# Attention and MoE on one core: batch 0's norms in one piece, batch 1's k and q cast and copied in other ways, pair 5's scores ahead of unit 4, the last values sooner

## The chip, the core and the metric

The kernel runs on one core of one Trainium2 chip. A core has five engines with a queue of their own, each working strictly in the order in which the program wrote its instructions: TensorE (PE, matrix products, with weight loads listed apart as PEld), VectorE (DVE), ScalarE (ACT), GpSimd (POOL) and SyncE (SP, which here only starts DMAs). They wait for each other by semaphores. Matrix products are written to PSUM banks; the other engines move them on to SBUF. The metric is the device time of one launch in microseconds (us); lower is better. The time before is 324.1 us, the median of three runs (323.36 to 324.86).

## The reference

Eight batches of eight heads, 576 positions, head size 64. First an attention with a window of 128 and a bias that falls with distance, then two matrix products with a gate between them:

```python
scores = scale * np.matmul(q, k.transpose(0, 1, 3, 2))
bias = slopes[:, None, None] * (-np.abs(rel).astype(np.float32))[None, :, :]
mask = (rel >= 0) & (rel < window)
scores = np.where(mask, scores + bias[None], -1000000000.0)
attn = np.exp(scores - np.max(scores, axis=-1, keepdims=True))
attn = attn / (np.sum(attn, axis=-1, keepdims=True) + 1e-09)
x = np.matmul(attn, v)              # then (8*576, 512): 4608 tokens
h = x @ w_in                        # (4608, 2048)
g = h * np.clip(h + 3.0, 0.0, 6.0) / 6.0
out = g @ w_out                     # (4608, 512), float32
```

## The kernel before

**Pairs.** The work of the attention goes by pairs of heads: pair g is heads 2p and 2p+1 of batch b, with g = 4b + p, 32 pairs in all. For batches 0 and 1 a pair's steps are:

- its k and q come in by DMA (`load_double`, two pairs at a time) as float32 in `ldbuf`; a cast to bf16 (`prepare_double`, L246, tile `pr`) is made in two halves, one for the even and one for the odd heads, on an engine that the caller names (V is VectorE, A ScalarE, P GpSimd);
- nine TensorE transposes turn two pairs' k, or q, into one PSUM tile. `wide_double` (L283 to L293) takes one of the two score tiles for it and moves both pairs on with one copy (1152 elements in a partition, L291, to `kTb` or `qTb`); `double` (L255) does it in two parts in other banks;
- `scores_diag` (L331) and `scores_off` (L357 and L363, after the bias tables L342 and L345) write the scores into one score tile each, `exp_diag` and `exp_off_full` (L407, L410, L394) take exponentials on ScalarE, and GpSimd masks what needs it (L412);
- `attend` multiplies by v (L440, L448) into a score tile; VectorE takes a reciprocal (L469) and multiplies by it (L470), which gives the normed values `avs`. `attend_split` does the same by two parts in two other banks, with two reciprocals and two products (L481, L482);
- `back` transposes `avs` on TensorE (L502) and copies the result into `xT`, the input of the first matrix product (L504, L505, L508). From batch 2 on, with two exceptions, a DMA transposes instead (L495).

There are only two score tiles, handed out in turn by `score_banks()`, so a user of one waits until the engine that reads its last content is done.

**Units.** The matrix products are cut into units, which `fill(n)` takes in order, n at a time, and which the program puts between the steps of the attention. An up unit (`moe_up`, four matmuls of 512 columns, L521) makes one 128 by 512 tile of h, ScalarE a relu of it (L545, tile `r`), VectorE the gate (L546, tile `gbuf`). Its PSUM bank comes from the pool "h" (two banks), or for some units of the first tile from "av" or "o" (one each, L535). A down unit (`moe_down`, L576) is a quarter of one 128-row block of the result. `up_begin` and `up_more` start units 0 and 1 of the first tile of tokens before all of `xT` is there. Units that need pairs that aren't done (`done[0]`) are not taken.

**Order.** Everything is in the order of the program text (`manual_schedule` for all engines). `first_batch` does batch 0 and prepares batch 1's first two pairs, `second_batch` does batch 1, and `segment` walks pairs 8 to 31 with a table of fills: at each pair seven numbers f[0] to f[6] say how many units go between which steps. At the last step, g = G = 32, only the values of pair 31 are left: `values` for blocks 0 to 2 (bank "av", reciprocal L458, product L459), `values` for blocks 3 and 4 in the same bank, and `back`, which is a DMA there. The tile of tokens number 7, the last but one, needs that DMA.

**Weights.** The first 512 columns of `w_in` come as float32 and are cast in four pieces (`cast_raw`, L187); the other three parts are DMAs that GpSimd issues (`load_w_in`, L176), the first of them in `second_w_in`.

The lines around the change, as numbered in the profile of the kernel before:

Of the kernel before, what the change touches and what calls it, by code (L numbers as in the profile page):

```python
# [11 lines left out]
BF16 = mybir.dt.bfloat16  # L12
# [6 lines left out]
def kernel(  # L19
# [9 lines left out]
    nc = tc.nc  # L29
    B, H, S, D = q.shape  # L30
# [5 lines left out]
    NP = H // 2  # L36
# [4 lines left out]
    RP, RT = 64, 9  # L41
# [5 lines left out]
    G = B * NP  # L47
# [5 lines left out]
    xT = perm.tile([128, n_ks, RING + SP - S], BF16)  # L53
# [12 lines left out]
    prs = ctx.enter_context(tc.tile_pool(name="prs", bufs=2))  # L66
# [119 lines left out]
    def cast_raw(ks, copy):  # L186
        copy(out=w_in_sb[:, ks, 0:512], in_=raw[:, ks, :])  # L187
# [33 lines left out]
    st = {}  # L221
# [20 lines left out]
    def prepare_double(b, dp, copies, nms="kq", early=None):  # L242
        for nm, copy in zip(nms, copies):
            pr = prs.tile([128, RT, 2 * D], BF16, tag=f"pr{nm}", name="pr2")
            for e in range(2):
                copy(out=pr[:, :, ts(e, D)],  # L246
                     in_=ldbuf["qk".index(nm)][:, ds((2 * dp + e) * RT * D, RT * D)].rearrange(
                         "p (t d) -> p t d", t=RT))
                if early and (nm, e) == (nms[0], 0):
                    early()  # L250
            st[b, dp, nm] = pr

    BANKS = {"h": ps_h, "av": ps_av, "o": ps_o}

    def double(b, dp, nm, part, tag, copy):  # L255
# [25 lines left out]
                         in_=st[b, dp, nm, part].rearrange("p t (a i) -> p i a t", i=2)[:, i])  # L281

    def wide_double(b, dp, nm, copy):  # L283
        src = st[b, dp, nm]
        wide = score_banks()
        tp = wide.rearrange("p s c -> p (s c)").bitcast(BF16)[:, 0:RT * 128].rearrange(
            "p (t c) -> p t c", t=RT)
        for t in range(RT):
            nc.tensor.transpose(tp[:, t, :], src[:, t, :], ident)
        dst = (qTb if nm == "q" else kTb)[b % 2][:, 2 * dp:2 * dp + 2, :, :]  # L290
        copy(out=dst.rearrange("p i j c -> p i (j c)")[:, :, 0:S].rearrange(  # L291
                 "p i (a t) -> p i a t", t=RT),
             in_=tp.rearrange("p t (a i) -> p i a t", i=2))  # L293

    def full(g):
        return g < NB_FULL * NP
# [176 lines left out]
    def attend_split(g, tags):  # L473
        st[g, "avs"] = small.tile([128, NQ, 2, D], BF16, tag="avs", name="avs")
        for tag, qts in zip(tags, ((0, 1, 2), (3, 4))):
            nq = len(qts)
            av = BANKS[tag].tile([128, 3, 2, W], FP32, tag=tag, name="av",
                                 padded_shape=[128, 3, 2, 85])
            av_matmuls(g, qts, lambda qt, e: av[:, qt - qts[0], e, :])
            rc = small.tile([128, 3, 2, 1], FP32, tag="rc", name="rc")  # L480
            nc.vector.reciprocal(rc[:, 0:nq, :, :], av[:, 0:nq, :, D:W])  # L481
            nc.vector.tensor_tensor(  # L482
                out=st[g, "avs"][:, qts[0]:qts[0] + nq, :, :], in0=av[:, 0:nq, :, 0:D],
                in1=rc[:, 0:nq, :, :].to_broadcast([128, nq, 2, D]), op=ALU.mult)
# [6 lines left out]
    def back(g, tag=None):  # L491
        b, hp = divmod(g, NP)
        avs = st[g, "avs"].rearrange("p j e d -> p j (e d)")
        if by_xbar(g):
            nc.sync.dma_start_transpose(  # L495
                out=xT[:, hp, ds(b % 4 * S, SP)].rearrange("p (j c) -> p j c", j=NQ),
                in_=avs.rearrange("p j c -> p (j c)"))
            return
        tag = tag or ("o" if b < 2 else "h")
        tp = BANKS[tag].tile([128, SP], BF16, tag=tag, name="tb", padded_shape=[128, 1024])  # L500
        for j in range(NQ):
            nc.tensor.transpose(tp[:, ts(j, 128)], avs[:, j, :], ident)  # L502
        if g == NP - 1:
            nc.scalar.copy(out=xT[:, hp, ds(b % 4 * S, 256)], in_=tp[:, 0:256])  # L504
            nc.vector.tensor_copy(out=xT[:, hp, ds(b % 4 * S + 256, S - 256)], in_=tp[:, 256:S])  # L505
            return
        eng = nc.vector.tensor_copy if g == 2 * NP - 1 else nc.scalar.copy
        eng(out=xT[:, hp, ds(b % 4 * S, S)], in_=tp[:, 0:S])  # L508

    gts, ops = {}, {}  # L510
# [19 lines left out]
    def up_more(nt, ms, n):  # L530
        hps, k0 = begun[nt, ms]
        up_mms(nt, ms, k0, n, hps)
        begun[nt, ms] = hps, n
# [99 lines left out]
    def first_batch():  # L633
        prepare(0, (V, A))
        load_block(0, "v", 1, nc.scalar)
        for j in (4, 0, 2, 3):
            load_block(0, "v", j, nc.sync)
        load_raw()
        warm_up(5)
        tables_diag(0)  # L640
        tables_off(0)
        transposes(0, (V, A))
        scores_diag(0)
        prepare(1, (P, V))
        transposes(1, (V, V))
        scores_off(0)
        exp_full(0)
        scores_diag(1)
        prepare_double(0, 1, (V, P), "qk")
        tables_off(1)  # L650
        scores_off(1)
        double_begin(0, 1, "q", ("av", "o"))
        double_begin(0, 1, "k", ("h", "h"))
        exp_full(1)
        double_copy(0, 1, "q", 0, (V, V))
        double_copy(0, 1, "k", 0, (A, A))
        scores_diag(2)
        double_copy(0, 1, "q", 1, (V, V))
        double_copy(0, 1, "k", 1, (V, V))
        tables_off(2)  # L660
        scores_off(2)
        exp_full(2)
        scores_diag(3)
        cast_v(0, 4, P)
        cast_v(0, 0, P)
        cast_v(0, 1, P)
        cast_v(0, 2, V)
        cast_v(0, 3, V)
        scores_off(3)
        exp_full(3)  # L670
        attend(0)
        for dp in range(2):
            for nm in "kq":
                load_double(1, dp, nm, nc.sync)
        load_tokens(1, "v")
        attend_split(1, ("av", "h"))
        attend(2)
        back(0, "o")
        cast_raw(0, P)
        cast_raw(1, P)  # L680
        attend(3)
        cast_raw(2, A)
        back(1, "av")
        cast_raw(3, P)
        prepare_double(1, 0, (P,), "k")
        second_w_in()
        up_begin(0, 0, 1)
        up_begin(0, 1, 1)
        back(2, "o")
        prepare_double(1, 0, (V,), "q")  # L690
        up_more(0, 0, 2)
        up_more(0, 1, 2)
        back(3, "av")
        wide_double(1, 0, "k", V)
        wide_double(1, 0, "q", A)
        up_more(0, 0, 3)
        up_more(0, 1, 3)
        done[0] = NP
        fill(2)
        prepare_double(1, 1, (P,), "k")  # L700
        load_w_in(2)
        prepare_double(1, 1, (P,), "q")
        load_w_in(3)
        for dp in range(2):
            for nm in "kq":
                load_double(2, dp, nm, nc.sync)

    def second_batch():
        scores_diag(NP + 0)
        exp_diag(NP + 0, 0)  # L710
        exp_diag(NP + 0, 1)
        fill(2)
        scores_off(NP + 0)
        exp_off_full(NP + 0)
        wide_double(1, 1, "k", V)
        wide_double(1, 1, "q", A)
        fill(2)
        scores_diag(NP + 1)
        exp_diag(NP + 1, 0)
        exp_diag(NP + 1, 1)  # L720
        fill(2)
        scores_off(NP + 1)
        exp_off_full(NP + 1)
        fill(1)
        cast_tokens(1, "v")
        scores_diag(NP + 2)
        exp_diag(NP + 2, 0)
        exp_diag(NP + 2, 1)
        fill(1)
        scores_off(NP + 2)  # L730
        exp_off_full(NP + 2)
        fill(2)
        for i in range(0, 4):
            load_w_out(i)
        g = 2 * NP - 1
        scores(g)
        exp_diag(g, 0)
        exp_diag(g, 1)
        prepare_double(2, 0, (V, P))
        prepare_double(2, 1, (P, P))  # L740
        nc.gpsimd.memset(ldbuf[2][:, 0:1], 0.0)
        load_tokens(2, "v")
        for dp in range(2):
            load_double(3, dp, "k", nc.sync)
        load_tokens(3, "q")
        exp_off_full(g)
        fill(1)
        attend(NP)
        fill(1)
        attend(NP + 1)  # L750
        fill(1)
        back(NP)
        attend(NP + 2)
        fill(1)
        back(NP + 1)
        double(2, 0, "k", 0, "av", A)
        attend(NP + 3)
        back(NP + 2)
        double(2, 0, "k", 1, "av", A)
        wide_double(2, 0, "q", A)  # L760
        up_begin(1, 0, 3)
        back(2 * NP - 1)
        up_begin(1, 1, 3)
        done[0] = 2 * NP
        fill(2)
        scores(2 * NP)

    FILLS = {g: (1, 1, 1, 2, 0, 1, 1) for g in range(9, 15)}

    def segment(lo, hi, fills):  # L770
        for g in range(lo, hi + 1):
# [91 lines left out]
```

## Time and profile before

| what | value |
|---|---|
| median of three runs | 324.1 us (323.36 to 324.86) |
| the profiled execution: its time | 323.67 us |
| its span, first to last instruction | 322.0 us |
| granted TensorE clock over the span | 0.999 |
| busy, share of the span: TensorE | 96% |
| VectorE, ScalarE, GpSimd | 54%, 61%, 43% |
| a relu (L545), a gate (L546), mean of 144 | 690 ns, 686 ns |
| a cast of 128 by 576 float32 (L246): VectorE, GpSimd | 746 ns, 671 ns |
| a copy of 1152 elements (L291): VectorE, ScalarE | 1350 ns, 1121 ns |
| a copy of 576 elements (L239): VectorE, ScalarE | 757 ns, 638 ns |
| L279, VectorE, every other element of a PSUM tile: 320 and 256 elements | 484 ns, 428 ns |

The busy time of an engine says little by itself: TensorE's matmuls are pipelined, and the end of each is modelled, so the starts of successive matmuls tell more than their durations. In a line of the timeline the first number is the start in us from the start of the span, the second how long the group took, and the bracket at the end how long the engine had been idle and what ended it. Instructions that follow each other on ScalarE or VectorE overlap a little: two relus of 0.69 us each take 1.27 us, and the next starts 1.15 us after the first.

### The profile page before, as it was taken

The numbers are of one execution on the slowest core, as the hardware profiler recorded it, in microseconds if no ns is written. First come the engines' busy times: TensorE is split into PE (matmuls) and PEld (weight loads), VectorE is DVE, ScalarE is ACT, GpSimd is POOL, SyncE is SP. The second block draws the span as 40 slices with busy tenths as digits, with TensorE's granted clock in tenths as the row PEclk, the third lists the DMA queues.
The fourth block names the chain that finished last, engine by engine and source line by source line (L and its number), as shares of the span: only waits on it lengthen the run. The fifth ranks groups of instructions, "written<-read, shape, count | busy, mean of one in ns | idle before, by whom it ended". The sixth has DMA issues, their size and how long they took to land.

```text
span 322.0 us, 7006 instructions
## 1 busy us (share of the span) xinstructions
PE 310.5 (96%) x2707; PEld 162.8 (51%) x2707; DVE 174.2 (54%) x345; ACT 197.0 (61%) x338; POOL 138.4 (43%) x247
## 2 busy tenths in 40 slices
PE   6888999999999999999999999999999999999996
PEld 3564465455555444444667644444444444444443
DVE  6776585555346655655555556555656355445510
ACT  3858977777777766766676667666764244244401
POOL 7365491666495666456754664563331000000000
PEclk9999999999999999999999999999999999999999
DMA  7999999989999998999899999943112100000112
GB/s 268 256 373 205 255 245 205 247 210 198 188 259 170 189 243 198 203 219 221 179 174 237 185 205 210 201 120 70 41 34 86 55 34 33 35 33 33 65 51 81
DMA packets 131425, 52.43 MB, mean 163 GB/s; under 512 B 118976, under 2 KB 122816, under 8 KB 131392
## 3 DMA queue, kind: packets, MB, share of 16 engines
q1 hardware_dynamic: 125648, 46.15, 67.3%
q0 software_dynamic: 3696, 3.67, 7.1%
q10 hardware_dynamic: 2048, 2.16, 2.2%
q8 instruction: 21, 0.34, 0.5%
q14 instruction: 12, 0.10, 0.1%
HBM read 36.70 MB, written 9.44 MB: 143 GB/s over the span
## 4 chain that ended last, share of the span: by engine, by line
PE 79%; DMA 7%; ACT 7%; DVE 4%; issue 2%; SPq 0%; DVEq 0%; ACTq 0%
PE ops L576 34%; PE hps L521 34%; PE score L384 3%; ACT r L545 3%; DMA ldbuf<-in_q_dram 3%; DMA xT<-avs 2%; DMA kTb<-tbuf 2%; PE av L448 2%; PE av L440 2%; PE ops L557 1%; DVE gbuf L546 1%; DVE avs L470 1%; ACT gbuf L410 1%; ACT gbuf L394 1%; PE tp L261 1%
## 5 line engine op out<-in xcount | busy, mean ns | idle before, releaser
L546 DVE SCALAR_TENSOR_TENSOR gbuf<-r,hps 128x512 bf16<-128x512 f32 x144 | 98.4, 686 | 103.5 <-ACT r L545 100.1
L545 ACT ACTIVATE r<-hps,bias 128x512 f32<-128x512 f32 x144 | 98.8, 690 | 87.6 <-PE hps L521 87.4
L521 PE MATMUL hps<-xT,w_in_sb 128*128 128x512 bf16 (+1 forms) x640 | 145.2, 358 | 1.4 <-DMA xT<-avs 0.8
L576 PE MATMUL ops<-w_out_sb,gbuf 128*128 128x512 bf16 x560 | 138.0, 379 | 0.0
L521 PEld LDWEIGHTS <-w_in_sb 128*128 128x128 bf16 x640 | 59.1, 98 | 55.7 <-issue 3.4
L576 PEld LDWEIGHTS <-gbuf 128*128 128x128 bf16 x560 | 52.2, 98 | 57.1
L412 POOL TENSOR_SCALAR_AFFINE_SELECT pd<-pd 128x512 bf16<-128x512 bf16 x48 | 29.5, 631 | 38.4 <-ACT pd L410 38.4
L421 POOL TENSOR_SCALAR_AFFINE_SELECT po<-po 128x512 bf16<-128x512 bf16 x48 | 30.1, 632 | 32.2 <-ACT po L419 32.0
L410 ACT ACTIVATE pd<-score,bias_d 128x512 bf16<-128x512 f32 x48 | 31.5, 683 | 5.7 <-PE score L384 5.7
L585 DVE COPY osb<-ops 128x512 f32<-128x512 f32 x33 | 22.7, 687 | 21.5 <-PE ops L576 21.4
L419 ACT ACTIVATE po<-score,bias_o 128x512 bf16<-128x512 f32 x48 | 33.1, 689 | 0.0
L213 POOL CAST tbuf<-ldbuf 128x512 bf16<-128x512 f32 (+1 forms) x45 | 25.5, 611 | 15.7 <-issue 15.7
L459 DVE TENSOR_TENSOR avs<-av,rc 128x384 bf16<-128x384 f32 (+1 forms) x48 | 23.6, 491 | 1.6
L448 PEld LDWEIGHTS <-pd 128*128 128x128 bf16 x192 | 14.3, 97 | 7.9 <-POOL tbuf L213 0.2
L440 PE MATMUL av<-vbuf,po 128*128 128x65 bf16 x192 | 18.0, 193 | 0.0
L448 PE MATMUL av<-vbuf,pd 128*128 128x65 bf16 x192 | 17.3, 193 | 0.0
L440 PEld LDWEIGHTS <-po 128*128 128x128 bf16 x192 | 14.3, 98 | 2.9 <-DVE avs L459 0.5
L424 ACT ACTIVATE p4buf<-score,bias_d 128x64 bf16<-128x64 f32 x48 | 15.6, 324 | 0.0
L206 POOL CAST vbuf<-ldbuf 128x1024 bf16<-128x1024 f32 x14 | 14.2, 1041 | 2.4 <-DMA ldbuf<-in_v_dram 2.4
L384 PEld LDWEIGHTS <-kTb 64*64 64x64 bf16 x480 | 9.4, 106 | 9.5 <-issue 8.5
L384 PE MATMUL score<-qTb,kTb 64*64 64x192 bf16 (+1 forms) x480 | 13.1, 234 | 0.3 <-DMA kTb<-tbuf 0.3
L246 POOL CAST pr<-ldbuf 128x576 bf16<-128x576 f32 x18 | 11.5, 671 | 3.2 <-DMA ldbuf<-in_k_dram 1.7
(108 smaller groups left out, 200.3 us busy)
## 6 DMA issues: line engine op xcount, KB each, us to landing
out_dram<-osb SPq DMA_DIRECT2D x33, 256.0 KB, 2.5
ldbuf<-in_v_dram SPq DMA_DIRECT2D x31, 256.0 KB, 4.9
ldbuf<-in_q_dram SPq DMA_DIRECT2D x20, 256.0 KB, 4.9
ldbuf<-in_k_dram SPq DMA_DIRECT2D x16, 256.0 KB, 4.8
ldbuf<-in_q_dram SPq DMA_DIRECT2D x12, 288.0 KB, 6.3
ldbuf<-in_k_dram SPq DMA_DIRECT2D x12, 288.0 KB, 6.4
w_out_sb<-in_moe_w_out_dram POOLq DMA_DIRECT2D x4, 512.0 KB, 10.5
w_in_sb<-in_moe_w_in_dram POOLq DMA_DIRECT2D x3, 512.0 KB, 10.1
```

The costliest lines, as they stand in the source:

```text
L213: nc.gpsimd.tensor_copy(out=tbuf[:m, :, j, :], in_=s[:m, j, :, :].rearrange("p (i e) d -> p i (e d)", e=2))
L384: nc.tensor.matmul(wide[e][c, ds(at, n)], lhsT=kT[r, j, c], rhs=qT[r, ds(q0, n)], start=True, stop=True)
L410: nc.scalar.activation(out=pd[:, e, :, :], in_=block_scores(g, e, False), func=ACT.Exp, bias=bias_d[:, h:h + 1], scale=scale)
L412: nc.gpsimd.affine_select(out=pd[:, e, :, :], in_=pd[:, e, :, :], pattern=[[0, 4], [1, 128]], channel_multiplier=-1, base=0, compare_op=AL ...
L419: nc.scalar.activation(out=po[:, e, :, :], in_=sc, func=ACT.Exp, bias=bias_o[:, h:h + 1], scale=scale)
L421: nc.gpsimd.affine_select(out=po[:, e, :, :], in_=po[:, e, :, :], pattern=[[0, 4], [-1, 128]], channel_multiplier=1, base=-1, compare_op=A ...
L440: nc.tensor.matmul(out_av, lhsT=po[:, e, (qt if full(g) else qt - 1) % 4, :], rhs=vb[:, qt - 1, h, :], start=True, stop=False)
L448: nc.tensor.matmul(out_av, lhsT=d, rhs=vb[:, qt, h, :], start=(qt == 0), stop=True)
L521: nc.tensor.matmul(hps[:, lo:hi], lhsT=w_in_sb[:, ks, ts(ms, 128)], rhs=xT[:, ks, ds(src, hi - lo)], start=(ks == 0), stop=(ks == n_ks - 1))
L545: nc.scalar.activation(out=r6, in_=hps, func=ACT.Relu, bias=bias3[:, 0:1], scale=1.0 / 6.0)
L546: nc.vector.scalar_tensor_tensor(out=gts[nt][:, ms, :], in0=r6, scalar=1.0, in1=hps, op0=ALU.min, op1=ALU.mult)
L576: nc.tensor.matmul(ops[nt, sub], lhsT=gts[nt][:, ms, ts(sub, 128)], rhs=w_out_sb[:, ms, :], start=(ms == 0), stop=(ms == n_ms - 1))
```

## The change

In `first_batch`: pair 1 is normed in one piece (`attend(1)`, in a score tile) and not by `attend_split`. The pieces of `w_in` are cast by P, A, A, P and not by P, P, A, P. The cast of batch 1's first q moves from VectorE (both halves) to ScalarE (even heads) and GpSimd (odd heads), in the new `prepare_halves`. Its first k and q are no longer copied two pairs at once: the new `wide_begin` does the nine transposes, and the new `wide_copy` moves one pair on, so that pair 4's k goes by VectorE and its q by ScalarE, and pair 5's k and q by VectorE after them. The k transposes stand before `back(3)`, which now copies on VectorE alone. In `second_batch`: the q of pairs 6 and 7 goes by `double` in two parts into banks "o" and "av", copied by VectorE and not by ScalarE; `scores_off(5)` follows `scores_diag(5)` directly, and the units 4 to 8 come after it in one row, where 4 and 5 stood before `scores_diag(5)`, 6 and 7 between the two and 8 behind. At the last step the fills are (1, 0, 1, 0, 0, 1, 2) and not (1, 1, 1, 2, 0, 1, 2): one unit instead of two before the values of blocks 0 to 2, and one instead of three between them and those of blocks 3 and 4. The units left out there come behind.

```diff
@@ first_batch
-        attend_split(1, ("av", "h"))
+        attend(1)
+        back(0, "o")
         attend(2)
-        back(0, "o")
         cast_raw(0, P)
-        cast_raw(1, P)
+        cast_raw(1, A)
+        back(1, "av")
         attend(3)
         cast_raw(2, A)
-        back(1, "av")
-        cast_raw(3, P)
         prepare_double(1, 0, (P,), "k")
         second_w_in()
         up_begin(0, 0, 1)
         up_begin(0, 1, 1)
         back(2, "o")
-        prepare_double(1, 0, (V,), "q")
         up_more(0, 0, 2)
         up_more(0, 1, 2)
+        wide_begin(1, 0, "k")
+        wide_copy(1, 0, "k", 0, 1, V)
+        prepare_halves(1, 0, "q", (A, P))
+        cast_raw(3, P)
         back(3, "av")
-        wide_double(1, 0, "k", V)
-        wide_double(1, 0, "q", A)
         up_more(0, 0, 3)
         up_more(0, 1, 3)
+        wide_begin(1, 0, "q")
+        wide_copy(1, 0, "q", 0, 1, A)
+        wide_copy(1, 0, "k", 1, 1, V)
+        wide_copy(1, 0, "q", 1, 1, V)
@@ second_batch
         wide_double(1, 1, "k", V)
-        wide_double(1, 1, "q", A)
-        fill(2)
+        double(1, 1, "q", 0, "o", V)
+        double(1, 1, "q", 1, "av", V)
         scores_diag(NP + 1)
         exp_diag(NP + 1, 0)
         exp_diag(NP + 1, 1)
-        fill(2)
         scores_off(NP + 1)
         exp_off_full(NP + 1)
-        fill(1)
+        fill(5)
@@ segment's fills
+    FILLS[G] = (1, 0, 1, 0, 0, 1, 2)
@@ the new functions
+    def prepare_halves(b, dp, nm, copies):
+        pr = prs.tile([128, RT, 2 * D], BF16, tag=f"pr{nm}", name="pr2")
+        for e in range(2):
+            copies[e](out=pr[:, :, ts(e, D)], in_=ldbuf[...])
+        st[b, dp, nm] = pr
+    def wide_begin(b, dp, nm):          # the transposes of wide_double
+        ...
+        st[b, dp, nm, "wide"] = tp
+    def wide_copy(b, dp, nm, i, n, copy):   # n pairs from pair i on
+        dst = (qTb if nm == "q" else kTb)[b % 2][:, ds(2 * dp + i, n), :, :]
+        copy(out=..., in_=st[b, dp, nm, "wide"].rearrange("p t (a i) -> p i a t", i=2)[:, ds(i, n)])
@@ back
-        if g == NP - 1:
-            nc.scalar.copy(out=xT[:, hp, ds(b % 4 * S, 256)], in_=tp[:, 0:256])
-            nc.vector.tensor_copy(out=xT[:, hp, ds(b % 4 * S + 256, S - 256)], in_=tp[:, 256:S])
-            return
-        eng = nc.vector.tensor_copy if g == 2 * NP - 1 else nc.scalar.copy
+        eng = nc.vector.tensor_copy if g in (NP - 1, 2 * NP - 1) else nc.scalar.copy
```

More of the change, by code (lines that the diff above doesn't have):

```diff
@@ L251, in prepare_double @@
             st[b, dp, nm] = pr
+    def prepare_halves(b, dp, nm, copies):
+        pr = prs.tile([128, RT, 2 * D], BF16, tag=f"pr{nm}", name="pr2")
+        for e in range(2):
+            copies[e](out=pr[:, :, ts(e, D)],
+                      in_=ldbuf["qk".index(nm)][:, ds((2 * dp + e) * RT * D, RT * D)].rearrange(
+                          "p (t d) -> p t d", t=RT))
+        st[b, dp, nm] = pr
     BANKS = {"h": ps_h, "av": ps_av, "o": ps_o}
@@ L283, in wide_double @@
     def wide_double(b, dp, nm, copy):
+        wide_begin(b, dp, nm)
+        wide_copy(b, dp, nm, 0, 2, copy)
+    def wide_begin(b, dp, nm):
         src = st[b, dp, nm]
@@ L289, in wide_double @@
             nc.tensor.transpose(tp[:, t, :], src[:, t, :], ident)
-        dst = (qTb if nm == "q" else kTb)[b % 2][:, 2 * dp:2 * dp + 2, :, :]
+        st[b, dp, nm, "wide"] = tp
+    def wide_copy(b, dp, nm, i, n, copy):
+        dst = (qTb if nm == "q" else kTb)[b % 2][:, ds(2 * dp + i, n), :, :]
         copy(out=dst.rearrange("p i j c -> p i (j c)")[:, :, 0:S].rearrange(
                  "p i (a t) -> p i a t", t=RT),
-             in_=tp.rearrange("p t (a i) -> p i a t", i=2))
+             in_=st[b, dp, nm, "wide"].rearrange("p t (a i) -> p i a t", i=2)[:, ds(i, n)])
     def full(g):
```

## The prediction

> **What bounds the kernel now.** I read the page's busy shares first, then the busy time by stretches, then each engine's timeline where TensorE (PE) pauses.
>
> ```profile
> PE 310.5 (96%) x2707; PEld 162.8 (51%) x2707; DVE 174.2 (54%) x345; ACT 197.0 (61%) x338; POOL 138.4 (43%) x247
> ```
> ```profile
> 17.00:24.20 7.20, 6.03 (x114) 4.58 (x115) 5.98 (x14) 3.66 (x7) 4.93 (x9) 1.00 1.07 369
> 24.20:32.00 7.80, 6.78 (x63) 3.68 (x61) 4.79 (x6) 6.82 (x10) 4.08 (x7) 1.00 1.25 205
> 32.00:42.00 10.00, 10.00 (x96) 4.74 (x94) 5.70 (x9) 9.98 (x17) 5.75 (x9) 1.00 1.14 278
> 245.00:254.00 9.00, 8.20 (x51) 3.79 (x48) 4.46 (x9) 1.96 (x3) 0.00 (x0) 1.00 0.18 53
> ```
>
> PE is the bound: a gain must come from its pauses, or from nowhere. In the second fence the columns are length, PE, PEld, DVE, ACT, POOL, clock, DMA share and GB/s. PE pauses in 17 to 32 us and near 250; from 32 to 42 ACT is full too (9.98 of 10 us). PE's timeline names the pauses:
>
> ```profile
> 23.71 0.68 PE L289 MATMUL score<-ident,pr 128*128 128x128 bf16 x9 [0.37 <-DVE pr L246]
> ...
> 25.60 0.40 PE L331 MATMUL score<-qTb,kTb 64*128 64x128 bf16 x8 [0.34 <-ACT qTb L291]
> ...
> 29.99 0.66 PE L289 MATMUL score<-ident,pr 128*128 128x128 bf16 x9 [0.68 <-ACT gbuf L394]
> ```
> ```profile
> 22.25 1.41 DVE L246 CAST pr<-ldbuf 128x576 bf16<-128x576 f32 x2
> ...
> 29.68 1.35 DVE L291 COPY kTb<-score 128x1152 bf16<-128x1152 bf16 x1
> ```
> ```profile
> 24.43 1.12 ACT L291 COPY qTb<-score 128x1152 bf16<-128x1152 bf16 x1 [1.17 <-PE score L289]
> ```
>
> The q transposes wait for DVE's cast, pair 4's scores for ACT's copy of both pairs, the second q transposes for a score tile. At the end:
>
> ```profile
> 249.12 0.17 DVE L458 RECIPROCAL rc<-av 128x4 f32<-128x4 f32 x1
> 249.32 0.42 DVE L459 TENSOR_TENSOR avs<-av,rc 128x256 bf16<-128x256 f32 x1
> ```
> ```profile
> 252.15 0.81 PE L521 MATMUL hps<-xT,w_in_sb 128*128 128x512 bf16 x3
> 253.76 1.24 PE L521 MATMUL hps<-xT,w_in_sb 128*128 128x512 bf16 x5 [0.80 <-DMA xT<-avs]
> ```
>
> Three matmuls start 0.215 us apart, so the fourth could start at 252.80 and starts at 253.76: 0.96 us lost, because the last norms end at 249.74 and their DMA takes 3.91.
>
> **Norms in one piece.** `attend(1)` now uses the score tile that pair 3's exponential (16.92 + 1.02) reads until 17.94: it starts at 17.99, not 17.63. DVE's split cost 1.24 us between starts (18.90 to 20.14), in one piece 1.06 (20.14 to 21.20). But pair 2's values now wait for pair 0's norms (18.98) and for `back(0)` (19.04 to 19.33), end at 20.07, and so start the third reciprocal at 20.12: the last norms end at 22.31 against 22.33. Worth nothing; bounds -0.02 and, by the late start, +0.36. I take nothing, as the next step shows cover.
>
> **First k and q.** POOL casts `w_in`'s piece 0 (18.75 to 19.36), then k's halves as they land (issued 12.72 and 14.4, 6.7 and 5.7 us to landing: 19.42, 20.1), done at 20.78; it issues the `w_in` DMA 0.9 us sooner, casts q's odd half when it has landed (15.7 + 6.0 = 21.7) by 22.42 and piece 3 by 22.97. Its next k cast waits for a DMA until 23.76 as before, so POOL is back in step. ACT copies pair 0 (19.53), casts piece 1 (0.62), copies pair 1 (20.60 to 21.24), casts piece 2, copies pair 2 (21.85 to 22.49) and casts q's even half (0.67, row L227) by 23.06. PE runs matmuls to 22.08, k transposes to 22.58, `back(3)`, two matmuls, and starts the q transposes at 23.30, not 23.71; the cast is ready 0.18 before, so this cover is thin. ACT's q copy for pair 4 alone (0.64, row L239) runs 24.02 to 24.66, not to 25.55. DVE, rid of the cast, copies pair 4's k from 22.80 (0.76), pair 3's `xT` (0.46) and pair 5's k to 24.62. Pair 4's scores start at 24.71, not 25.60: **-0.89**. DVE's q half is queued behind and waits for ACT's half of the same tile: 24.71 to 25.47, and the gate of unit 0 behind that ends at 26.08. Unit 3 needs its bank and stops PE for 0.24 (0.13 before, from 26.79 to about 26.92): +0.12, leaving -0.77 at `scores_off(4)` (27.00).
>
> The trace has DVE's second half of a copy after ACT's first (L279, 12.67 to 13.46, then 13.64), but DVE was busy until 13.7, so it decides nothing. The Trainium skill, page PSUM — Partial Sum Buffer, section PSUM bank collisions raise a hardware error, says that two engines must not read one bank at once, so halves on two engines come one after the other. By that rule the wait stands as in my sum; if the halves ran together, the gate would end 0.11 sooner (then the relu before it decides) and the sum would be 0.1 better; no run here shows it yet.
>
> **Second q and pair 5's scores.** ACT loses a copy (1.01 between starts) and reaches pair 4's off exponential at 28.03, end 29.08. PE ends both transposes by 28.87; bank "av" is free in time (gate of unit 2 ends 28.27). `scores_diag(5)` needs that exponential's tile: 0.26 idle. `scores_off(5)` needs the second k copied: DVE does it after unit 3's gate (28.85), 28.77 to 30.12. PE idles from 29.46 to 30.17: 0.70. These pauses together, 0.96, stand where 0.85 was lost before (29.14 to 29.99). Then five units in a row: unit 7 needs unit 4's bank (gate ends 33.56, needed 33.62), unit 8 its weights, a DMA issued at 24.37 that takes 10.1 us, so 34.5, needed 34.48. Pair 6's scores come at 35.45 after the usual 0.1 pause of a mode change, not 36.22. ACT then limits until 42: unit 12's relu at 42.13 against 42.85, and the wait for pair 4's norms follows it. Carried on: **-0.73**. DVE's two q copies (0.73 for 512 elements, row L263, so some 0.84 for the part of 640) end near 31.5 and hide before unit 4's gate at 32.87; units 5 and 8, which take the banks they empty, come at 31.9 and 34.5. Without that cover each us of excess costs one. The bounds of this part: no gain if the pauses grow by 0.73, and -1.7 if they vanish.
>
> After 49 us SP's DMA queue stands free before 70.59, waiting for norms, so it shifts along; I carry the gain to the end in full.
>
> **Last values.** One unit less before the first values: 243.83, not 244.69. Their norms follow the gate of the unit before (243.89 + 0.69): reciprocal 244.50, product 244.72 to 245.28. PE has one unit (to 245.00) and then idles to 245.34: +0.34, like the row where values wait 0.51 for L459 at 90.17. On SP the last DMA passes one output DMA (0.34 to issue), for which nothing waits. The second norms follow that unit's gate (245.93 to 246.62) and end at 247.17, not 249.74; the DMA lands near 251.2. PE arrives at 252.50 and doesn't wait: -0.96 + 0.34 = **-0.62**. Bounds: 0 and -0.96.
>
> **Sum.** -0.73 - 0.62 = -1.35. The profiled execution took 323.67 (span 322.0), so 322.3; the median stands 0.43 above it, so I predict **322.7**, 0.4% faster. About 0.5% (1.62 us, to 322.5) is what a measurement of this kernel can tell from no change.
>
> **Rivals.**
> - *One half is given back.* PE already waits 0.33 for a `kTb` DMA at 114.14, and SP issues without a gap from 82.99 to 106.41. If that train doesn't move, PE waits 0.73 more and only the end counts: 323.5. Against: the train starts after a DMA that waits for norms (81.73). If instead the end fails, 323.4.
> - *The pauses at 29 and 245 are shorter.* ACT is lighter by one copy and DVE's gates may come sooner. Without the 0.96 the first part gives -1.7, cut by ACT's full stretch to about -1.3, and the end -0.62: 322.2, at best 321.4 with -0.96.
> - *Slower: unit 8 waits for its weights.* It comes 0.76 sooner, on a DMA that lands just then, with PE's queue behind it. Each us late costs one; past 35.8 the gain is gone, past 37.5, 13 us after issue, the kernel is 0.5% slower. For: a v load of this stretch took 14.2; at that, 38.6, PE waits 4.1 and the time is 326.8. Against: this one took 10.1, and the `w_in` DMA ahead of it starts sooner.
> - *The change doesn't do what it says:* the end still waits, because the second norms stay behind a late gate, and the pauses at 29 eat the first gain: 324.1. Against: both gates are placed by rows above.
>
> **How the numbers follow.** Forecast 0.47, one half given back 0.15, shorter pauses 0.27, slower 0.06, nothing 0.05. The forecast's own range is 322.2 to 323.2. From 321.6 (pauses nearly gone) to 324.2 (one half lost, the runs spread 0.76) less than 2 in 10 is left out. Faster by over 0.5%: shorter pauses and an eighth of the forecast, 0.33; slower 0.06; the rest, 0.61, within.
>
> **What would show it.** Right: pair 4's first L331 near 24.7; a pause of 0.7 before L342 near 30; units 4 to 8 without pauses; no wait for `xT<-avs` near 252 but one of 0.3 before L440 near 245. Wrong: the q transposes waiting for ACT's or POOL's cast; unit 8's weight load waiting for a DMA; a longer wait for `kTb` near 113.

## The result, and the profile after

The changed kernel takes 322.51 us (median of four runs, 322.27 to 322.54) against 324.48 for the kernel before on the same chip (323.36 to 325.08): a ratio of 0.994, interval 0.991 to 0.9969. Timed again later, on one chip with two of its variants, it took 322.98 against 324.40: 0.9955, interval 0.9942 to 0.9968, which is 1.46 us less (1.04 to 1.88). I had forecast 322.7, from a time before of 324.1, and a sum of -1.35. The profiled execution took 322.52, span 320.8.

Lines of the changed file stand 8 to 15 lower than those of before: the scores of pairs 4 and 5 are now L346 and L357 (331 and 342), values L455 and L463 (440 and 448), `wide_copy` L306, the cast in `prepare_halves` L256, products of norms L485 and L474 (470 and 459), the up matmuls L532 (521), the scores from pair 8 on L399 (384).

First the table by stretches of the changed kernel (columns as in the prediction's second fence).

```profile
core 0: us, PE busy (x) PEld busy (x) DVE busy (x) ACT busy (x) POOL busy (x), PEclk, DMA share, GB/s
32.00:42.00 10.00, 10.00 (x96) 4.92 (x94) 6.82 (x10) 9.36 (x15) 5.22 (x7) 1.00 0.99 240
42.00:113.00 71.00, 69.34 (x667) 36.35 (x665) 40.22 (x78) 52.15 (x95) 44.90 (x79) 1.00 1.10 218
245.00:254.00 9.00, 9.00 (x50) 4.15 (x47) 4.22 (x8) 2.53 (x5) 0.00 (x0) 1.00 0.20 61
```

PE fills the last stretch now (9.00 of 9.00, 8.20 before), and ScalarE has some room between 32 and 42 (9.36, 9.98 before). The long row is one that the prediction did not use: from 42 to 113 us PE is busy for 69.34 of 71.00, but the 16 DMA engines are full as well (share 1.10).

TensorE's timeline at the front of the changed kernel, and VectorE's and ScalarE's beside it:

```profile
22.79 0.67 PE L301 MATMUL score<-ident,pr 128*128 128x128 bf16 x9
...
24.19 0.40 PE L346 MATMUL score<-qTb,kTb 64*128 64x128 bf16 x8
...
28.58 0.40 PE L346 MATMUL score<-qTb,kTb 64*128 64x128 bf16 x8
29.68 0.32 PE L357 MATMUL score<-tab,ident 128*128 128x384 bf16 x1 [0.70 <-DVE kTb L306]
```
```profile
22.29 0.76 DVE L306 COPY kTb<-score 128x576 bf16<-128x576 bf16 x1 [0.57 <-PE score L301]
22.96 0.45 DVE L519 COPY xT<-tb 128x576 bf16<-128x576 bf16 x1
23.32 0.75 DVE L306 COPY kTb<-score 128x576 bf16<-128x576 bf16 x1
24.17 0.76 DVE L306 COPY qTb<-score 128x576 bf16<-128x576 bf16 x1
```
```profile
21.88 0.68 ACT L256 CAST pr<-ldbuf 128x576 bf16<-128x576 f32 x1
23.50 0.64 ACT L306 COPY qTb<-score 128x576 bf16<-128x576 bf16 x1 [0.94 <-PE score L301]
```

The q transposes no longer wait on VectorE's cast, pair 4's scores start right after ScalarE's shorter copy (23.50 + 0.64 = 24.14), and the one pause left is the 0.70 that was forecast, for the copy of the second k. Pair 4's scores come at 24.19 and not at 25.60, 1.41 sooner. Of this 0.43 is no gain, as this execution was early before anything was changed: the first norms' product starts at 17.73, in the kernel before at 18.16. That leaves 0.98 against the 0.89 forecast.

TensorE's later waits, and its end, in the changed kernel:

```profile
113.14 0.55 PE L399 MATMUL score<-qTb,kTb 64*64 64x192 bf16 x20 [0.57 <-DMA kTb<-tbuf]
...
124.93 1.24 PE L532 MATMUL hps<-xT,w_in_sb 128*128 128x512 bf16 x5 [0.42 <-DMA xT<-avs]
...
244.80 0.20 PE L455 MATMUL av<-vbuf,po 128*128 128x65 bf16 x1 [0.16 <-DVE avs L474]
...
251.96 1.89 PE L532 MATMUL hps<-xT,w_in_sb 128*128 128x512 bf16 x8
```

At 251.96 eight matmuls go in one row: the wait of 0.96 is gone. Ahead of 244.80 stands the small pause that replaces it (four matmuls of 0.86 in all from 243.61, so 0.33 idle). At 113 and 125 there are two waits for DMAs, 0.57 and 0.42, where the kernel before showed 0.33 and none. Set against the kernel before, TensorE is 1.25 us ahead at 52 us, 1.00 behind the first of these waits, 0.62 behind the second, 0.53 at 235, and 1.2 at the end. Was the first part's gain given back there, or not?

### The profile page after: what moved, and what is told of

Its sections match the earlier page's. It is cut to its first block, busy times and chain, and to the rows that moved or that the text cites. A ratio compares the mean times of both kernels' runs of the same rounds, so it can differ in the third digit from the quotient of the medians.

```text
span 320.8 us, 7007 instructions
## 1 busy us (share of the span) xinstructions
PE 309.9 (97%) x2707; PEld 162.8 (51%) x2707; DVE 175.3 (55%) x345; ACT 196.7 (61%) x338; POOL 138.9 (43%) x247
## 4 chain that ended last, share of the span: by engine, by line
PE 61%; DMA 4%; issue 2%; POOL 1%; ACT 1%; DVE 0%; POOLq 0%
PE ops L587 29%; PE hps L532 26%; DMA kTb<-tbuf 2%; PE score L399 2%; PE av L463 1%; DMA xT<-avs 1%; PE av L455 1%; PE ops L568 1%; POOL tbuf L213 1%; ACT r L556 0%; POOL pd L427 0%; DMA qTb<-tbuf 0%; ACT po L434 0%; DVE avs L474 0%; DVE gbuf L557 0%
## 5 line engine op out<-in xcount | busy, mean ns | idle before, releaser
L532 PE MATMUL hps<-xT,w_in_sb 128*128 128x512 bf16 (+1 forms) x640 | 144.7, 358 | 1.0 <-DMA xT<-avs 0.4
L532 PEld LDWEIGHTS <-w_in_sb 128*128 128x128 bf16 x640 | 59.2, 98 | 55.5 <-issue 2.7
L474 DVE TENSOR_TENSOR avs<-av,rc 128x384 bf16<-128x384 f32 (+1 forms) x48 | 23.6, 491 | 1.6
L463 PEld LDWEIGHTS <-pd 128*128 128x128 bf16 x192 | 14.3, 97 | 7.8 <-POOL tbuf L213 0.2
L455 PE MATMUL av<-vbuf,po 128*128 128x65 bf16 x192 | 18.0, 193 | 0.2 <-DVE avs L474 0.2
L463 PE MATMUL av<-vbuf,pd 128*128 128x65 bf16 x192 | 17.3, 194 | 0.0
L455 PEld LDWEIGHTS <-po 128*128 128x128 bf16 x192 | 14.3, 98 | 3.4 <-DVE avs L474 1.2
L399 PEld LDWEIGHTS <-kTb 64*64 64x64 bf16 x480 | 9.4, 106 | 9.8 <-issue 8.0
L399 PE MATMUL score<-qTb,kTb 64*64 64x192 bf16 (+1 forms) x480 | 13.1, 234 | 0.6 <-DMA kTb<-tbuf 0.6
```

The costliest lines, as they stand in the source:

```text
L399: nc.tensor.matmul(wide[e][c, ds(at, n)], lhsT=kT[r, j, c], rhs=qT[r, ds(q0, n)], start=True, stop=True)
L455: nc.tensor.matmul(out_av, lhsT=po[:, e, (qt if full(g) else qt - 1) % 4, :], rhs=vb[:, qt - 1, h, :], start=True, stop=False)
L463: nc.tensor.matmul(out_av, lhsT=d, rhs=vb[:, qt, h, :], start=(qt == 0), stop=True)
L532: nc.tensor.matmul(hps[:, lo:hi], lhsT=w_in_sb[:, ks, ts(ms, 128)], rhs=xT[:, ks, ds(src, hi - lo)], start=(ks == 0), stop=(ks == n_ks - 1))
```

## The experiments

To compare the traces of the variants I use one table. The first column is the start of the first norms' product (VectorE, L470 or L485), up to which all the programs are the same. The second is the distance from there to the first matmul of pair 8's scores (50.7 to 52.5 us), so it holds the front part alone and not the chance of the start. Then the waits by the timeline's brackets, and the distance from the first product to pair 18's scores (near 130). All in us.

| kernel | first product | to pair 8 | wait near 114, 125 | to pair 18 | wait near 252 |
|---|---|---|---|---|---|
| before | 18.16 | 33.87 | 0.33, none | 112.26 | 0.80 |
| before_again | 18.59 | 33.87 | 0.73, none | 112.69 | 0.79 |
| tail_alone | 18.43 | 33.86 | none, 0.63 | 112.44 | none |
| before_late | 18.32 | 33.89 | none, none | 112.03 | 0.91 |
| first_alone | 18.63 | 33.02 | 0.54, 0.43 | 112.00 | 0.48 |
| second_alone | 18.11 | 34.05 | none, 0.26 | 112.27 | 1.02 |
| front_alone | 17.65 | 33.18 | 1.05, 0.68 | 112.92 | none |
| norms_split | 17.53 | 33.18 | 0.41, 0.33 | 111.95 | none |
| after | 17.73 | 33.05 | 0.57, 0.42 | 112.07 | none |
| after_again | 18.47 | 33.05 | 0.30, 0.35 | 111.71 | none |
| delay | 17.69 | 33.92 | none, 0.40 | 112.13 | none |
| later_units | 18.42 | 33.05 | none, none | 111.18 | none |
| all_mended | 18.53 | 32.63 | none, none | 110.76 | none |
| mended_w_in | 18.44 | 32.29 | none, none | 110.42 | none |

The variants ran on three chips. Timed differences below are against the kernel before, timed beside them on the same chip, with the 95% interval of the ratio turned into us by its median.

### The end alone

The kernel before, with

```diff
+    FILLS[G] = (1, 0, 1, 0, 0, 1, 2)
```

> The kernel before with only the last fills changed. Theory A (the steps as predicted): the last DMA of norms no longer makes TensorE wait near 252 (-0.96), TensorE idles 0.3 to 0.35 before the last values near 245, so -0.6 against the kernel before, and everything ahead of 240 us stays as it was, the wait of 0.33 for kTb near 114 too. Theory B (the end only looks better because it comes later than the first part's gain): 0 to -0.2. Theory C (the DMA of the norms is paced by other transfers, not by its issue): it lands as late as before and the wait near 252 stays, 0.

Measured: 323.68 against 324.51, 0.9972 (0.9952 to 0.9992), so -0.9 (-1.6 to -0.3). TensorE takes eight matmuls in a row at 252.94, without the wait. Theory A stands; B and C are excluded, though the interval is wide. The front is as before, and yet in this execution the wait near 114 was gone and the one near 125 was 0.63, where theory A had them stay: the first sign that these waits are no property of the change.

### The front alone, and its first part alone

The changed kernel without the line above (`front_alone`), and also with `second_batch` as before (`first_alone`).

> The changed kernel with the last fills as before, so only the work of batches 0 and 1 is changed. Theory A (the gain of the first part is carried on): TensorE is 0.8 ahead at 52 us and at the end, -0.8 against the kernel before. Theory D (the DMA queue that SyncE feeds doesn't move): in the changed kernel SyncE issued the transfer behind batch 2's norms at 70.57, against 70.59 before, though TensorE was 1.25 ahead; so TensorE waits longer for kTb near 113 (0.57 there, 0.33 before) and for xT near 125 (0.42, none before), and of the 0.8 only 0 to 0.3 is left behind 126: -0.1 to -0.3 against the kernel before. The wait of about 0.9 for xT near 252 is there by both.

> The changed kernel with second_batch and the last fills as before: norms in one piece, the first k and q cast by other engines and copied by pair, nothing else. By the prediction's steps pair 4's scores come 0.9 sooner and the pause before the second q transposes near 29 grows, because ScalarE's order there is unchanged: between -0.1 and -0.8 at 52 us. Theory A carries this to the end (-0.1 to -0.8); theory D leaves at most 0.2 of it behind the waits near 113 and 125.

Measured: `front_alone` 322.97, 0.9949 (0.9927 to 0.9972), so -1.7 (-2.4 to -0.9); `first_alone` 323.78, 0.9981 (0.9959 to 1.0002), so -0.6 (-1.3 to +0.1). Theory D gave -0.1 to -0.3 for `front_alone`, which the times exclude; theory A's -0.8 lies just outside the interval too. The interval of `first_alone` holds both theories. The pause near 29, which I expected to grow there, is 0.60 against 0.68 before, so at 52 us this kernel is 0.85 ahead. But `front_alone`'s profile shows D's mechanism at its strongest (TensorE's timeline):

```profile
113.66 0.55 PE L399 MATMUL score<-qTb,kTb 64*64 64x192 bf16 x20 [1.05 <-DMA kTb<-tbuf]
...
125.71 1.24 PE L532 MATMUL hps<-xT,w_in_sb 128*128 128x512 bf16 x5 [0.68 <-DMA xT<-avs]
```

By the table this execution lost more behind 52 us than its front had gained (112.92 against 112.26), got 0.8 back because the wait near 252 was hardly there this time (no bracket; the eight matmuls take 2.04 and not 1.89, so 0.15), and took 323.02. One profile is not enough to say where the gain of 0.7 to 0.8 goes. In the same trace the weight load of the q transposes waits 0.46 for GpSimd's cast; the front stretch is 0.13 longer than in the changed kernel, and in `first_alone`, which started a microsecond later and does not wait there, it is not.

### The kernel before, profiled again

> The kernel before, looked at once more. Theory F (the time before 17 us and the DMA waits differ from execution to execution): the product of the first norms, at 18.16 in the first look, lies anywhere between 17.6 and 18.7, as it does in the five other kernels' traces, all of which have the same program up to there; the waits for kTb near 114 (0.33), for xT near 125 (none) and near 252 (0.80 in the page's words) come out otherwise and add up to more than 1.1, since the first look was 0.8 under the median of this kernel's runs. Theory G (the first look is typical in its steps): the same three waits within 0.1.

```profile
114.96 0.55 PE L384 MATMUL score<-qTb,kTb 64*64 64x192 bf16 x20 [0.73 <-ACT r L545]
...
254.62 1.24 PE L521 MATMUL hps<-xT,w_in_sb 128*128 128x512 bf16 x5 [0.79 <-DMA xT<-avs]
```

The releaser named in the first line is not the one that counts: in the first profile the same scores started at 114.14, while that relu ran until 114.53. The DMA of `kTb` was issued at 107.42 here, and 7.5 us later, within what the executions show (6.9 to 8.4 from issue to landing), is 114.9. So theory F: a start later by 0.43 and a longer wait for the same DMA (0.73 against 0.33) make up 0.83 of the 0.88 between this execution's 324.55 and the first one's 323.67. Timed, the kernel took 324.73 beside 324.40 for itself (1.0004, 0.9993 to 1.0016). The front stretch is 33.87 in both, to the hundredth. The first profile, on which the prediction rests, was an early one with a short wait.

### Extra work, and the changed kernel on the same chip

`after_again` is the changed kernel; `delay` has one line more:

```diff
         fill(2)
+        warm_up(4)
         scores(2 * NP)
```

> The changed kernel on the same chip as its variants: the sum predicted is -1.35 against the kernel before; theory D, with the first part's gain lost to the DMA waits, gives -0.7; the first measurement gave -2.0.

> The changed kernel with four more matmuls of 128 by 512 on TensorE at about 50 us, 0.86 us of work whose result nothing reads. Theory A (TensorE is the bound throughout): +0.86. Theory D (between 50 and 125 us the DMA sets the time): the waits of 0.57 near 113 and 0.42 near 125 take it up, 0 to +0.2 at the end.

Measured: `after_again` 322.98, -1.46 (-1.88 to -1.04), which holds the forecast -1.35 and not theory D's -0.7; `delay` 324.49 against the same 324.40, ratio 1.0 (0.9983 to 1.0017). The 0.86 us of extra work cost 1.5 (0.8 to 2.2, from the two intervals). Theory D's 0 to +0.2 is out; A's 0.86 lies inside, near the low end. The trace of `delay` is of its fastest execution (322.80, the median is 324.49) and looks more like theory D. It shows the work in the front stretch (33.92 against 33.05, +0.87), no wait near 114 and one of 0.40 near 125, so that at pair 18 only 0.42 of it is left against `after_again` and 0.06 against `after`. By the times, time lost ahead of these DMAs is lost, on the average of many runs, even where a single profile shows waits that take part of it up. Why the median rose by 1.5 and not by 0.86 is not shown.

### Taking the DMA waits away

The changed kernel (`later_units`) and the kernel before (`before_late`), each with

```diff
+    FILLS[15], FILLS[16] = (1, 1, 1, 2, 0, 1, 3), (0, 1, 1, 1, 0, 2, 2)
```

> The changed kernel with pair 15's fills (1, 1, 1, 2, 0, 1, 3) and pair 16's (0, 1, 1, 1, 0, 2, 2): one unit more ahead of pair 16's scores, which wait for kTb near 113, and one less ahead of pair 15's last values, whose norms the DMA carries that is waited for near 125. Theory D: both waits go (0.57 and 0.42 in the changed kernel), the lead of the first part lasts to 240, and the time falls by 0.5 to 0.9 against the changed kernel, to about 321.8. Theory E (the whole DMA train is late, so that the next transfer is waited for instead): the wait moves to another pair, 0 to -0.3. Theory A has no give-back to mend: 0.

> The kernel before with only the fills of pairs 15 and 16 changed as in later_units, the front and the end untouched. Theory J (the DMA waits near 114 and 125 are there in most executions of either kernel, 0.33 and 0.73 at the first place in two looks at the kernel before): -0.3 to -0.8. Theory D (they are the price of the changed kernel's earlier start): 0 to -0.3.

Measured: `later_units` 322.42, 0.9941 (0.9917 to 0.9964), -1.9 (-2.7 to -1.2); `before_late` 323.34, 0.9965 (0.9941 to 0.9989), -1.1 (-1.9 to -0.4). The kernel before gains too, so the waits are there in either kernel, as theory J has it; theory D's -0.3 lies just outside. The time of `later_units` does not bear out theory D's 321.8: its -1.9 cannot be told from the changed kernel's own -1.46, which was timed on another chip. In the traces the waits are gone and come up at no other pair, which is against theory E; the distance to pair 18 falls by 0.53 and 0.89 against the two profiles of the changed kernel. The scores of pair 16 in `later_units`, without a bracket:

```profile
114.04 0.55 PE L399 MATMUL score<-qTb,kTb 64*64 64x192 bf16 x20
117.76 0.20 PE L455 MATMUL av<-vbuf,po 128*128 128x65 bf16 x1 [0.17 <-DVE avs L474]
121.56 0.55 PE L399 MATMUL score<-qTb,kTb 64*64 64x192 bf16 x20
```

The scores of pairs 8 and 18 in `before_late`, then in `later_units`:

```profile
52.21 0.55 PE L384 MATMUL score<-qTb,kTb 64*64 64x192 bf16 x20
...
130.35 0.55 PE L384 MATMUL score<-qTb,kTb 64*64 64x192 bf16 x20
```
```profile
51.47 0.55 PE L399 MATMUL score<-qTb,kTb 64*64 64x192 bf16 x20
...
129.60 0.55 PE L399 MATMUL score<-qTb,kTb 64*64 64x192 bf16 x20
```

These traces settle what became of the front's gain, which the times of the two, on two chips and with overlapping intervals, could not. With the waits out of both, the two kernels differ by 0.84 at pair 8 (33.89 and 33.05) and by 0.85 at pair 18 (112.03 and 111.18), and it is still 0.85 at the last scores, those of pair 31. The gain is carried in full; what the first profiles showed as given back is a DMA that lands a few tenths sooner or later from one execution to the next.

### The second part alone, and the norms

`second_alone` is the kernel before with `second_batch` as changed; `norms_split` the changed kernel with

```diff
-        attend(1)
-        back(0, "o")
+        attend_split(1, ("av", "h"))
         attend(2)
+        back(0, "o")
```

> The kernel before with only second_batch changed: the second q in two banks by VectorE, pair 5's two score steps in a row, five units behind them. By the prediction's steps the pauses there come to 0.96 against 0.85 before, so +0.1 at 52 us and in the time; the traces of first_alone and after_again (0.85 and 0.82 ahead at 52 us, from equal starts) say 0.0 likewise. Theory I (the medians, not the steps: the first part alone gave -0.7 and both parts -1.5): this part alone gives about -0.8.

> The changed kernel with pair 1 normed by two parts again and the transposes of pair 0 behind pair 2's values, as before. The prediction took the norms in one piece for worth nothing (bounds -0.02 and +0.36): then this kernel's q transposes stand at the same distance from its first norms as in the changed kernel (5.06 us from the first product to the q transposes, 22.79 - 17.73), and the time is the same, within 0.2. Rival: the last norms end 0.17 sooner in the changed kernel than forecast, relative to its start, because of that edit; then this kernel loses 0.1 to 0.4.

Measured: `second_alone` 324.80 against 324.05, 1.0015 (0.9995 to 1.0034), +0.5 (-0.2 to +1.1); `norms_split` 322.71, 0.9949 (0.9927 to 0.997), -1.7 (-2.4 to -1.0). TensorE's pauses in `second_alone`:

```profile
29.95 0.40 PE L331 MATMUL score<-qTb,kTb 64*128 64x128 bf16 x8 [0.18 <-ACT gbuf L394]
31.05 0.32 PE L342 MATMUL score<-tab,ident 128*128 128x384 bf16 x1 [0.70 <-DVE kTb L291]
```

The second part by itself makes the front stretch 0.18 longer (34.05); behind the first part it costs 0.03 (33.02 to 33.05). Theory I is out: by this, the larger gap between the medians of `first_alone` and the whole change was chance.

For the norms the prediction's zero holds within 0.2 by the trace; the times can't tell the kernels apart. But it is not quite zero. VectorE's last norms and TensorE's k transposes, in `norms_split`:

```profile
20.82 0.82 DVE L485 TENSOR_TENSOR avs<-score,rcw 128x640 bf16<-128x640 f32 x1
```
```profile
21.47 0.67 PE L301 MATMUL score<-ident,pr 128*128 128x128 bf16 x9
```

From the first product the norms end at 4.11 here and at 3.98 in the changed kernel, and the k transposes start at 3.94 and 3.85 (21.58 - 17.73). So 0.09 of the 0.13 by which the stretch of `norms_split` is longer stands ahead of the q transposes and goes with the norms, as the rival has it, at the low edge of its 0.1 to 0.4. `front_alone` has the same 0.13, for another reason: its k transposes start at 3.85, and the q transposes follow them by 1.34, in the changed kernel by 1.21 and in `norms_split` by 1.23.

### The pauses that are left

`all_mended` is `later_units` with a unit over each of the two pauses:

```diff
         exp_diag(NP + 1, 1)
+        fill(1)
         scores_off(NP + 1)
         exp_off_full(NP + 1)
-        fill(5)
+        fill(4)
...
-    FILLS[G] = (1, 0, 1, 0, 0, 1, 2)
+    FILLS[G] = (1, 0, 2, 0, 0, 1, 1)
```

and `mended_w_in` is that with

```diff
-        prepare_double(1, 0, (P,), "k")
-        second_w_in()
+        prepare_double(1, 0, (P,), "k", early=second_w_in)
```

> The changed kernel with three more edits: the units of pairs 15 and 16 as in later_units; one of the five units between pair 5's two score steps, over the pause of 0.70; one unit more between the last two values, over the pause of 0.33. Theory H (PE's own pauses add up once the DMA waits are out of the way): 0.5 at 31 us, since ScalarE is nearly full there, 0.5 at 113 to 125, 0.3 at 245, so 1.3 less than the changed kernel, near 321.2. Theory D in its strict form (kTb and xT land when the DMA lets them, whatever TensorE does before): the 0.5 at 31 us comes back as waits near 114 and 125, leaving 0.5 + 0.3 = 0.8 less, near 321.7.

> The kernel all_mended, but GpSimd issues the second quarter of w_in between its two casts of the first k instead of behind them, 0.7 us sooner. Theory H: in all_mended unit 4 waits 0.48 for that transfer (issued 20.77, taking 9.4); landing 0.7 sooner takes the wait away, ScalarE is nearly full from there on and keeps half of it: -0.2 to -0.4 against all_mended (321.5). Theory K (the transfer is paced by those ahead of it, not by its issue): it lands as late as before and nothing is gained; the second k cast, 0.4 later, may delay the k transposes by up to 0.2: 0 to +0.2.

Measured: `all_mended` 321.49, 0.9923 (0.9895 to 0.9951), -2.5 (-3.4 to -1.6), span 319.9; `mended_w_in` 322.04, 0.9943 (0.9924 to 0.9962), -1.9 (-2.5 to -1.2), span 319.5. The traces fit theory H: the front stretch falls by 0.42 and by another 0.34, no DMA is waited for near 114 or 125, and the end loses nothing any more. The unit put over the pause of 0.70 met a wait of its own in `all_mended`:

```profile
30.27 0.81 PE L532 MATMUL hps<-xT,w_in_sb 128*128 128x512 bf16 x3 [0.48 <-DMA w_in_sb<-in_moe_w_in_dram]
```

In `mended_w_in` GpSimd issues that transfer at 20.53 and not at 20.77, and the wait is gone. But this is 0.24 sooner and not the 0.7 I expected, as GpSimd's first cast started later there (19.04 and 18.62); and the transfer took 8.6 us there and 9.2 in `all_mended` (9.4 in the expectation). So one trace each does not show that it was the edit that took the wait away, and theory K stays open. The times bear the gain out only partly. `all_mended` is the fastest median here, 1.5 under the changed kernel beside it on the same chip (321.49 and 322.98), but the two intervals overlap; `mended_w_in` has the shortest trace, and its timed ratio, from another chip, cannot be told from the changed kernel's. All that is sure is that both beat the kernel before.

## Why the prediction was right, step by step

**Norms in one piece, worth nothing.** Too low by about 0.1, and outside the bound of -0.02. The last norms end 3.98 after the first product begins, forecast 4.15 (22.31 - 18.16), since one pair's norms take 0.98 from product to product and not 1.06. I took the next step to cover what they gain or lose; by `norms_split` 0.09 of it reaches the k transposes.

**First k and q, -0.77.** Measured -0.85 in `first_alone`, norms and all; the 0.08 more is the size of what the norms gave. From the first product, pair 4's scores come at 6.46 (24.19 - 17.73), forecast 6.55; pair 4's table scores at 8.70, forecast 8.84, before 9.61. The cover I called thin is thin, as the weight load of the q transposes shows, in the changed kernel and in `front_alone`:

```profile
22.67 0.61 PEld L301 LDWEIGHTS <-pr 128*128 128x128 bf16 x9 [0.21 <-POOL pr L256]
```
```profile
22.84 0.51 PEld L301 LDWEIGHTS <-pr 128*128 128x128 bf16 x9 [0.46 <-POOL pr L256]
```

In the changed kernel GpSimd's cast ends at 22.49 (21.83 + 0.66), 0.18 before the load, as forecast. The 0.21 of idle time is no wait for it: the same 0.21 stands there in `after_again`, where the cast ended 0.79 before, and the q transposes come 5.06 after the first product in both. In `front_alone`, which started earlier (17.65), the cast ended 0.06 before the load, and the front cost 0.13 more. That is the first of my signs for a wrong forecast, at a small size.

VectorE's q half starts at 24.17, 0.03 after ScalarE's half of the same tile has ended, and in `front_alone` its bracket names that copy (0.24 idle). The rule of the Trainium skill (PSUM — Partial Sum Buffer, section PSUM bank collisions raise a hardware error) and the trace agree so far as the order goes: the halves came one after the other, as in my sum. But it is the program that waits on a semaphore here, so no run shows what the chip does without it.

**Second q and pair 5's scores, +0.04.** Right: the pause of 0.70 is there to the hundredth, the one ahead of `scores_diag(5)` too (28.58, with the transposes' last start near 28.3), units 4 to 8 run without a pause and unit 8's weights come in time; +0.03 behind the first part, +0.18 alone. The +0.04 is the forecast's step from -0.77 to -0.73. Its two pauses by themselves (0.96 for 0.85) would make it +0.11; the rows of pair 6 (35.45 for 36.22) and unit 12 (42.13 for 42.85) give the rest back, and the prediction names no reason.

**Carried to the end in full.** Right on the average, for a reason that was only half right. I argued that SyncE's queue stands free before 70.59, waiting for norms. In the first profile of the changed kernel it did not: that transfer was issued at 70.57, straight behind an output that had waited for loads (69.90). In `after_again` it did stand free: the output came at 68.19, the transfer at 70.08. From 42 to 127 us the DMA engines are full (share 1.06 before, 1.10 after), and TensorE's arrival at `kTb` and `xT` is a race in every execution. The rival in which half of the gain is given back, for which I had 0.15, is what the first profile showed and what the rest does not bear out: the times of `after_again`, `front_alone` and `delay` exclude theory D, and without the waits 0.84 is carried as 0.85.

**The end, -0.62.** Exactly that in the first profiles: from the down unit at 241.24 to that at 254.84 before, 13.60; from 240.71 to 253.69 after, 12.98. Its worth varies all the same, since the wait it removes was between 0.15 and 1.02 in the kernels that still had it, against a pause of 0.33 or 0.34 in every execution with these fills. Timed alone it gave -0.9 (-1.6 to -0.3).

**The sum and its base.** Forecast -1.35, measured -1.46 (-1.88 to -1.04), and -1.95 (-2.9 to -1.0) in the first comparison. The base was the weaker half. I added 0.43 to the profiled time because the median stood so far above it; the second profile shows what such a difference is made of, 0.43 at the start and 0.4 at one DMA. That 322.7 came so near to the 322.51 of the first comparison is partly luck: the kernel before took 324.48 there, from which the sum gives 323.1. By that comparison the change is 0.6% faster, an outcome beyond 0.5%, to which I gave 0.33; by the later one it is 0.45%.

## What to carry to other kernels

A single trace gives the cost of a local step to some 0.1 us if it is measured from a point just ahead of the step, not from the start of the span. Where a full DMA stage follows, the same trace tells little of how much of a gain arrives: take the waits out of both kernels and compare again, or delay the kernel on purpose and time it. And before a wait for a DMA is blamed on a change, profile the kernel before a second time.

## What the runs showed of the hardware

- With the same program up to there, the first norms' product started anywhere from 17.53 to 18.63 in the executions of the table, a spread of 1.10 us, nearly as large as the effect measured here. From that point to pair 8's scores, two executions of one kernel agreed to 0.01 (33.87 twice, 33.05 twice); `front_alone`, with the changed kernel's program up to there, took 33.18.
- The same DMA transposition (`kTb<-tbuf`) took 6.9 to 8.4 us from issue to landing in the fourteen profiles, amid full DMA engines, and TensorE's wait for it was anything from none to 1.05.
- The bracket of a line can name the wrong releaser: the relu put down for the 0.73 us at 114.96 was still running when the same matmul started in another execution.
